# Batch 0's scaling on one engine, A^T in two steps, and one run of small tiles fewer, in a cross-attention and Gelu MLP kernel

## The chip, the cores and the metric

The kernel runs on one core of a Trainium2 chip. The metric is the time on the device in microseconds; the profile shows a single execution, and its times count from the start of that execution. The core's engines are named as in the profile: PE is TensorE (matrix products; PEld is its loading of weights), DVE is VectorE, ACT is ScalarE, POOL is GpSimd and SP is SyncE, which here only issues transfers.

## The reference

Two stages are computed. The first is cross-attention between x (8 batches, 8 heads, 512 rows of 64) and a state (32 rows of 64 for each head), in both directions. The second is an MLP with an exact Gelu on all rows of the result.

```python
scores = scale * np.matmul(x, state.transpose(0, 1, 3, 2))
a = softmax(scores)                       # written out: max, exp, sum, divide
xread = np.matmul(a, state)
scores2 = scale * np.matmul(state, x.transpose(0, 1, 3, 2))
a2 = softmax(scores2)
sread = np.matmul(a2, x)
attn = np.concatenate([xread, sread], axis=2)
# ... heads side by side: 4352 rows of 512
h = attn @ w_in                           # 512 x 2048
g = 0.5 * h * (1.0 + erf(h / sqrt(2)))
out = g @ w_out                           # 2048 x 512, float32
```

## The kernel before

xread is never formed. For each batch the kernel builds P, the product of the block-diagonal state (sbd) and w_in, and then takes `h = A @ P`, with A the scaled attention weights of all heads. P has 2 halves (t) by 2048 columns, built in chunks of 512 columns. The products of a chunk are small tiles: eight of 64x32, each with 512 columns. Everything else on TensorE uses the whole 128x128 array or has its own shapes.

The parts that matter here, cut; `...` marks cuts. The order of the calls is the order of the instructions on each engine.

```python
ps_f = ...tile_pool(name="ps_f", bufs=4, space=PSUM)     # tag "f": four PSUM banks in rotation
ps_o = ...tile_pool(name="ps_o", bufs=1, space=PSUM)     # tags o0 to o3: four banks, taken by turn

def otile(shape, name, at=None):
    if at is None:
        at = turn[0] % 4
        turn[0] += 1
    return ps_o.tile(shape, FP32, name=name, tag=f"o{at}")

def keep_warm(n):                       # products whose result nobody reads
    ps = otile([128, 512], "warm_ps")
    for _ in range(n):
        nc.tensor.matmul(ps[:, 0:128], lhsT=warm, rhs=warm, start=True, stop=True)

load_w_in(0, 256); load_w_in(256, 512)  # two transfers each, issued by GpSimd
load_w_out(0, 2); load_w_out(2, 4)
load_w_in(512, 1024)
load_st(1, 2)                           # state of batch 1

def norm0(t):                           # batch 0: A = e / sum, half t
    nc.vector.reciprocal(out=ics, in_=A.sums)
    eng = nc.gpsimd if t == 0 else nc.vector
    eng.tensor_tensor(out=..., in0=..., in1=ics..., op=ALU.mult)

def atr(b, ts=(0, 1)):                  # A^T through TensorE and PSUM
    ...
    for t in ts:
        ps = ps_f.tile([128, SJ, 128], BF16, name="aT_ps", tag="f")
        for j in range(SJ):
            nc.tensor.transpose(ps[:, j, :], A.a[:, 2 * j + t, :], ident)
        nc.vector.tensor_copy(out=A.AT[:, :, t, :], in_=ps)

def p_copy(b, f, ps):                   # a chunk of P: half 0 by ScalarE, half 1 by VectorE
    nc.scalar.copy(out=dst[:, 0, :], in_=ps[0])
    nc.vector.tensor_copy(out=dst[:, 1, :], in_=ps[1])

def pmat(b, f): ...                     # the products of one chunk, then p_copy
def burst(chunks): ...                  # the products of all chunks in one run, then the copies in order
def pmat00(h): ...                      # 256 columns of batch 0's chunk 0; both copies by ScalarE
def ones0(q): ...                       # VectorE copies for sread
def state_prep(b0, b1): ...             # transposes the states into sbd: TensorE, then VectorE
# M(m): two products A^T by P (line 481) and one Gelu by ScalarE
# mm2_m(0, m): four products g by w_out for batch 0 (line 534); U(u): four for later rows (line 507)

# the head
norm0(0); load_x(1); scores0(3); sums0(2); sums0(3); norm0(1)
load_rest()
keep_warm(2);  pmat00(0)
keep_warm(2);  pmat00(1)
nc.scalar.activation(out=gate, in_=gate, func=AF.Gelu)    # brings in the Gelu table early
keep_warm(10); atr(0, (0,))
keep_warm(3);  atr(0, (1,))
for q in range(4): ones0(q)
hps = [ps_f.tile(..., name="hp", tag="f") for m in range(4)]
for t in range(2):
    for m in range(4):
        nc.tensor.matmul(hps[m], lhsT=Ps[0][:, t, m*128:(m+1)*128], rhs=atts[0].AT[:, :, t, :], ...)
for m in range(4):
    nc.scalar.activation(out=gs[0][:, m, :], in_=hps[m], func=AF.Gelu)
turn[0] = 3
for m in range(3): mm2_m(0, m)
pmat(0, 1)
mm2_m(0, 3); M(4, 5); state_prep(1, 2); M(6)
...
pmat(0, 2) ... burst([(0, 3), (1, 0)]) ... burst([(1, 1), (1, 2)])
... burst([(1, 3), (2, 0), (2, 1)]) ... pmat(2, 2) ... pmat(2, 3)
```

After batch 2 the kernel goes through a steady loop, which the change leaves alone.

Of the kernel before, what the change touches and what calls it, by code (L numbers as in the profile page):

```python
# [10 lines left out]
BF16 = mybir.dt.bfloat16  # L11
# [6 lines left out]
def kernel(  # L18
# [8 lines left out]
    nc = tc.nc  # L27
# [8 lines left out]
    SJ = S // 128  # L36
# [11 lines left out]
    ps_f = ctx.enter_context(tc.tile_pool(name="ps_f", bufs=4, space=PSUM))  # L48
    ps_o = ctx.enter_context(tc.tile_pool(name="ps_o", bufs=1, space=PSUM))
# [3 lines left out]
    turn = [0]  # L53
# [6 lines that stand above are left out]
# [29 lines left out]
    for q in range(4):  # L89
        eng = nc.scalar if q == 2 else nc.sync  # L90
# [12 lines left out]
    def load_w_in(f0, f1):  # L103
        for t in range(2):
            nc.gpsimd.dma_start(  # L105
                out=w_in_bf[64 * t:64 * t + 64, :, f0:f1],
                in_=moe_w_in[256 * t:256 * t + 256, f0:f1].rearrange("(c d) f -> d c f", c=HC),
            )
# [3 lines left out]
    def load_w_out(m0, m1):  # L112
        nc.gpsimd.dma_start(out=w_out_bf[:, m0:m1, :], in_=w_out_r[:, m0:m1, :])
# [6 lines left out]
    def load_st(b0, b1):  # L120
        nc.gpsimd.dma_start(
            out=st_bf[:, b0:b1, :, :].rearrange("q b t d -> q (b t) d"),
            in_=st_rows[:, b0:b1, :, :].rearrange("q b t d -> q (b t) d"),
        )

    load_w_in(0, 256)
    load_w_in(256, 512)
    load_w_out(0, 2)
    load_w_out(2, 4)
    load_w_in(512, 1024)  # L130
    load_st(1, 2)


    def load_rest():
# [11 lines left out]
    def keep_warm(n):  # L146
# [5 lines that stand above are left out]
    def state_prep(b0, b1):  # L152
        n = b1 - b0
        ps = ps_f.tile([128, n, HC, NS], BF16, name="st_ps", tag="f")
        for b in range(b0, b1):
            nc.tensor.transpose(
                ps[:, b - b0, :, :].rearrange("p c n -> p (c n)"),
                st_bf[:, b, :, :].rearrange("q t d -> q (t d)"),
                ident,
            )  # L160
        for t in range(2):
            nc.vector.tensor_copy(
                out=sbd[64 * t:64 * t + 64, b0:b1, :, 32 * t:32 * t + 32].rearrange(
                    "d b c n -> d (b c) n"
                ),
                in_=ps[64 * t:64 * t + 64, :, :, :].rearrange("d b c n -> d (b c) n"),
            )
# [76 lines left out]
    def ones0(q):  # L244
        nc.vector.tensor_copy(
            out=atts[0].xo[:, :, q % 2 * 2:q % 2 * 2 + 2, 2 + q // 2 * 64:66 + q // 2 * 64],
            in_=x0b[:, q, :, :, :],
        )
# [58 lines left out]
    def norm0(t):  # L307
        A = atts[0]
        ics = att.tile([128, SJ, HC], FP32, name="ics", tag="ics")
        nc.vector.reciprocal(out=ics, in_=A.sums)  # L310
        eng = nc.gpsimd if t == 0 else nc.vector
        eng.tensor_tensor(
            out=A.a.rearrange("p (j t) (c n) -> p j t c n", t=2, n=NS)[:, :, t, :, :],
            in0=A.e.rearrange("p (j t) (c n) -> p j t c n", t=2, n=NS)[:, :, t, :, :],
            in1=ics[:, :, :].to_broadcast((128, SJ, HC, NS)),
            op=ALU.mult,
        )
# [39 lines left out]
    def atr(b, ts=(0, 1)):  # L357
        A = atts[b]
        if 0 in ts:
            A.AT = att.tile([128, SJ, 2, 128], BF16, name="AT", tag="AT")  # L360
        for t in ts:
            ps = ps_f.tile([128, SJ, 128], BF16, name="aT_ps", tag="f")
            for j in range(SJ):
                nc.tensor.transpose(ps[:, j, :], A.a[:, 2 * j + t, :], ident)
            nc.vector.tensor_copy(out=A.AT[:, :, t, :], in_=ps)

    def atr_dma(b):
        A = atts[b]
# [6 lines left out]
    def sread(b):  # L375
        A = atts[b]
        A.sr = ftile([128, 2, 65], "sr")
        for t in range(2):
            for j in range(SJ):
                for c in range(HC):  # L380
                    nc.tensor.matmul(  # L381
                        A.sr[32 * c:32 * c + 32, t, :],
                        lhsT=A.e[:, 2 * j + t, 32 * c:32 * c + 32],
                        rhs=A.xo[:, j, c, 1 + 65 * t:66 + 65 * t],
                        start=(j == 0),
                        stop=(j == SJ - 1),
                    )

    def sread_out(b):
        A = atts[b]  # L390
        A.srm = att.tile([128, 2, D], BF16, name="srm", tag="srm")
        flat = A.sr.rearrange("q t d -> q (t d)")
        inv = att.tile([128, 2], FP32, name="inv", tag="inv")
        nc.vector.reciprocal(out=inv, in_=flat[:, 0:130:129])
        nc.vector.tensor_tensor(
            out=A.srm,
            in0=flat[:, 1:129].rearrange("q (t d) -> q t d", t=2),
            in1=inv[:, :].to_broadcast((128, 2, D)),
            op=ALU.mult,
        )  # L400
# [11 lines left out]
    def p_mm(b, f, tiles):  # L412
        if b not in Ps:
            Ps[b] = att.tile([128, 2, d_ff], BF16, name="P", tag="P")
        ps = [tiles([128, 512], "p_ps") for t in range(2)]
        for c in range(HC):
            for t in range(2):
                nc.tensor.matmul(  # L418
                    ps[t][32 * c:32 * c + 32, :],
                    lhsT=sbd[64 * t:64 * t + 64, b, c, 32 * t:32 * t + 32],  # L420
                    rhs=w_in_bf[64 * t:64 * t + 64, c, f * 512:(f + 1) * 512],
                    start=True,
                    stop=True,
                )
        return ps

    def p_copy(b, f, ps):
        dst = Ps[b][:, :, f * 512:(f + 1) * 512]
        nc.scalar.copy(out=dst[:, 0, :], in_=ps[0])  # L429
        nc.vector.tensor_copy(out=dst[:, 1, :], in_=ps[1])  # L430

    def pmat(b, f):
        p_copy(b, f, p_mm(b, f, ftile))
# [4 lines left out]
    def burst(chunks, b_read=None):  # L438
        done = []
        first = len(chunks) < 4 and b_read is not None  # L440
        if first:
            sread(b_read)
        for i, (b, f) in enumerate(chunks):
            done.append((b, f, p_mm(b, f, ftile if i < 2 else otile)))
        for x in done[:2]:
            p_copy(*x)
        if b_read is not None and not first:
            sread(b_read)
        for x in done[2:3]:
            p_copy(*x)  # L450
        if b_read is not None:
            sread_out(b_read)
        for x in done[3:]:
            p_copy(*x)
# [75 lines left out]
    def mm2_m(b, m):  # L530
        for j in range(SJ):
            if m == 0:
                ops[b, j] = otile([128, d_model], "op")
            nc.tensor.matmul(  # L534
                ops[b, j],
                lhsT=gs[b][:, m, j * 128:(j + 1) * 128],
                rhs=w_out_bf[:, m, :],
                start=(m == 0),
                stop=(m == MC - 1),
            )  # L540
# [268 lines left out]
    def M(*ms):  # L809
        for m in ms:  # L810
            mm1(m // MC, m % MC)

    def U(*us):
        for u in us:
            mm2(u // 16, u % 16 // 4, u % 4)
# [28 lines left out]
    load_rest()  # L844
    keep_warm(2)
    pmat00(0)
    keep_warm(2)
    pmat00(1)
    nc.scalar.activation(out=gate, in_=gate, func=AF.Gelu)
    keep_warm(10)  # L850
    atr(0, (0,))
    keep_warm(3)
    atr(0, (1,))
    for q in range(4):
        ones0(q)

    gs[0] = gpool.tile([128, MC, S], BF16, name="g", tag="g")
    hps = [ps_f.tile([128, S], FP32, name="hp", tag="f") for m in range(4)]  # L860
    for t in range(2):
        for m in range(4):
            nc.tensor.matmul(  # L863
                hps[m],
                lhsT=Ps[0][:, t, m * 128:(m + 1) * 128],
                rhs=atts[0].AT[:, :, t, :],
                start=(t == 0),
                stop=(t == 1),
            )
    for m in range(4):  # L870
        nc.scalar.activation(out=gs[0][:, m, :], in_=hps[m], func=AF.Gelu)
    turn[0] = 3
    for m in range(3):
        mm2_m(0, m)
    pmat(0, 1)
    mm2_m(0, 3)
    M(4, 5)
    state_prep(1, 2)
    M(6)
    begin(1)  # L880
    xtr(1, (0, 1))
# [18 lines left out]
    M(10, 11)  # L900
    mm2_m(0, 8)
    mm2_m(0, 9)
    burst([(0, 3), (1, 0)])
    mm2_m(0, 10)
    atr(1)
    M(12, 13)
# [5 lines left out]
    xtr_dma(2)  # L912
    rearr_ones(2)
    U(12)
    burst([(1, 1), (1, 2)])
    U(13)
    state_prep(2, B)
    M(16, 17)
    U(14)
    M(18, 19)  # L920
    U(15)
    burst([(1, 3), (2, 0), (2, 1)])
    U(16)


# [2 lines left out]
    nc.gpsimd.tensor_copy(out=hold, in_=gs[1][:, 4, 0:1])  # L928
    load_x(4)
    w_sums(0)  # L930
    pmat(2, 2)
    begin(3)
    rearr(3)
    xtr_dma(3)
# [97 lines left out]
    b = B - 1  # L1032
# [40 lines left out]
```

The softmax here doesn't subtract the row's maximum and nothing guards it: scores larger than these inputs give would overflow.

## Time and profile before

| | |
|---|---|
| time, median of 3 runs | 206.2 us (206.19 to 206.49) |
| profiled execution | 205.62 us, span 203.8 us |
| busy: PE, DVE, ACT, POOL | 97%, 66%, 65%, 32% of the span |
| granted TensorE clock | 1.00 |
| scaling of batch 0, half 0 (POOL) | 9.08 us, 1.09 long |
| scaling of batch 0, half 1 (DVE) | 9.44 us, 1.28 long |
| the eight hp products of batch 0's first chunk | from 11.39 us |
| first Gelu | 12.66 us |

The profile lists, for each engine, what it did and when, and what ended the idle time ahead of an instruction. The chain of work that ended last is followed back from the end: at each step to whatever released it. Where that chain is on one engine without a gap, only less work on this engine, or an earlier start, makes the kernel shorter. The ends of matrix products are modelled, so the distance between the starts of groups says more than the length of one product.

### The profile page before, as it was taken

How to read it: one execution, taken by the hardware profiler on the slowest of the kernel's cores; microseconds unless marked ns; L12 is line 12 of the kernel's file. 1: busy time of each engine (PE TensorE's matmuls, PEld its weight loads, DVE VectorE, ACT ScalarE, POOL GpSimd, SP SyncE). 2: the span in 40 equal slices, each digit the busy share in tenths (PEclk: the TensorE clock that was granted, in tenths of full speed). 3: DMA queues.
4: the chain of work that ended last, by engine and by line, in shares of the span. 5: the costliest groups of instructions: out<-in, count | busy, mean ns of one | idle time of the engine just before them, and what ended most of it. 6: DMA issues, size and time to landing. Idle time of an engine off the chain costs nothing.

```text
span 203.8 us, 4714 instructions
## 1 busy us (share of the span) xinstructions
PE 197.9 (97%) x1972; PEld 131.2 (64%) x1979; DVE 134.0 (66%) x219; ACT 133.3 (65%) x240; POOL 65.9 (32%) x73
## 2 busy tenths in 40 slices
PE   8799999999999999999999999999999999999994
PEld 7445444444444577766776687567775887778893
DVE  2944675776758649876797767765778543165883
ACT  3774875589894879566967596678857376744120
POOL 8984610755060315360527502420220011200000
PEclk9999999999999999999999999999999999999999
DMA  6999999789575908782783306340109001030125
GB/s 195 192 176 202 206 199 193 127 236 124 127 96 155 204 11 106 156 180 29 89 170 142 69 0 140 124 102 3 53 37 172 3 0 51 3 154 0 55 100 159
DMA packets 40325, 23.14 MB, mean 114 GB/s; under 512 B 21872, under 2 KB 38384, under 8 KB 40304
## 3 DMA queue, kind: packets, MB, share of 16 engines
q1 hardware_dynamic: 25616, 14.36, 29.2%
q0 software_dynamic: 14000, 8.10, 29.1%
q10 hardware_dynamic: 688, 0.39, 0.6%
q8 instruction: 15, 0.25, 0.5%
q14 instruction: 6, 0.05, 0.1%
HBM read 17.30 MB, written 8.91 MB: 129 GB/s over the span
## 4 chain that ended last, share of the span: by engine, by line
PE 93%; DMA 2%; POOL 2%; issue 0%; DVE 0%; POOLq 0%
PE xp L589 35%; PE hp L481 27%; PE op L507 8%; PE op L534 5%; PE p_ps L418 5%; PE hps L521 3%; PE rp L765 3%; DMA w_in_bf<-in_moe_w_in_dram 2%; PE xp L695 2%; PE pt L327 2%; PE sr L381 1%; POOL w_in_bf L105 1%; PE hp L863 1%; POOL sbd L95 1%; PE xT_ps L267 1%
## 5 line engine op out<-in xcount | busy, mean ns | idle before, releaser
L488 ACT ACTIVATE g<-hp 128x512 bf16<-128x512 f32 x124 | 67.0, 602 | 27.4 <-PE hp L481 21.9
L481 PE MATMUL hp<-AT,P 128*128 128x512 bf16 x248 | 63.6, 379 | 0.1
L589 PEld LDWEIGHTS <-gsum 128*128 128x128 bf16 x448 | 43.4, 98 | 11.1 <-issue 1.9
L583 DVE TENSOR_TENSOR gsum<-g 128x2048 bf16<-128x2048 bf16 x30 | 38.6, 1307 | 0.1
L481 PEld LDWEIGHTS <-P 128*128 128x128 bf16 x248 | 22.8, 98 | 20.8 <-issue 2.5
L589 PE MATMUL xp<-ws,gsum 128*128 128x256 bf16 x256 | 30.6, 273 | 0.0
L430 DVE CAST P<-p_ps 128x512 bf16<-128x512 f32 x31 | 20.1, 686 | 10.6 <-PE p_ps L418 10.5
L589 PE MATMUL xp<-ws,g 128*128 128x256 bf16 x192 | 22.9, 273 | 0.0
L589 PE MATMUL xp<-w_out_bf,gsum 128*128 128x256 bf16 x192 | 22.8, 273 | 0.0
L429 ACT CAST P<-p_ps 128x512 bf16<-128x512 f32 x31 | 16.9, 597 | 7.4 <-PE p_ps L418 7.2
L589 PEld LDWEIGHTS <-g 128*128 128x128 bf16 x192 | 18.8, 98 | 4.3
L638 POOL TENSOR_TENSOR u<-s,oh 128x512 f32<-128x512 f32 x5 | 6.6, 1311 | 41.0 <-ACT oh L635 41.0
L507 PE MATMUL op<-w_out_bf,g 128*128 128x512 bf16 x76 | 19.0, 379 | 0.1
L231 POOL COPY xo<-xb 128x1024 bf16<-128x1024 bf16 x12 | 14.5, 1240 | 12.6 <-PE sr L381 12.6
L221 POOL COPY x<-xb 128x1024 bf16<-128x1024 bf16 x12 | 12.3, 1056 | 8.5 <-DMA xb<-in_x_dram 8.5
L608 POOL TENSOR_TENSOR v<-q,oh 128x512 f32<-128x512 f32 x5 | 7.1, 1428 | 20.8 <-ACT oh L640 20.8
L507 PEld LDWEIGHTS <-g 128*128 128x128 bf16 x80 | 7.6, 98 | 9.6 <-issue 0.8
L347 DVE TENSOR_REDUCE cs<-e 128x16 f32<-128x512 bf16 x14 | 9.5, 678 | 3.4 <-ACT e L334 3.4
L534 PE MATMUL op<-w_out_bf,g 128*128 128x512 bf16 x45 | 11.4, 380 | 0.2
L632 DVE TENSOR_TENSOR s<-xp,s 128x512 f32<-128x512 f32 x5 | 3.5, 692 | 11.3 <-PE xp L589 11.3
L350 DVE TENSOR_TENSOR a<-e,ics 128x512 bf16<-128x512 bf16 x14 | 10.3, 738 | 0.5
L418 PE MATMUL p_ps<-w_in_bf,sbd 64*32 64x512 bf16 x248 | 10.4, 382 | 0.1
(111 smaller groups left out, 220.3 us busy)
## 6 DMA issues: line engine op xcount, KB each, us to landing
xb<-in_x_dram POOLq DMA_DIRECT2D x7, 512.0 KB, 7.4
out_dram<-oh SPq DMA_DIRECT2D x13, 256.0 KB, 2.4
out_dram<-osb SPq DMA_DIRECT2D x10, 256.0 KB, 3.4
out_dram<-oh SPq DMA_DIRECT2D x5, 512.0 KB, 2.8
w_out_bf<-in_moe_w_out_dram POOLq DMA_DIRECT2D x8, 256.0 KB, 9.7
w_in_bf<-in_moe_w_in_dram POOLq DMA_DIRECT2D x6, 256.0 KB, 10.1
x0f<-in_x_dram SPq DMA_DIRECT2D x3, 256.0 KB, 3.8
w_in_bf<-in_moe_w_in_dram POOLq DMA_DIRECT2D x4, 128.0 KB, 4.1
```

What stands on the lines that cost most here:

```text
L221: nc.gpsimd.tensor_copy(out=A.x4[:, :, :, 64 * t:64 * t + 64].rearrange("p j c d -> p c j d"), in_=src[:, t],)
L231: eng.tensor_copy(out=A.xo[:, :, :, 2 + 64 * t:66 + 64 * t].rearrange("p j c d -> p c j d"), in_=src[:, t],)
L350: nc.vector.tensor_tensor(out=A.a[:, :, hs].rearrange("p g (c n) -> p g c n", n=NS), in0=e4, in1=ics[:, :, :].to_broadcast((128, G, 2, NS) ...
L418: nc.tensor.matmul(ps[t][32 * c:32 * c + 32, :], lhsT=sbd[64 * t:64 * t + 64, b, c, 32 * t:32 * t + 32], rhs=w_in_bf[64 * t:64 * t + 64, c ...
L429: nc.scalar.copy(out=dst[:, 0, :], in_=ps[0])
L430: nc.vector.tensor_copy(out=dst[:, 1, :], in_=ps[1])
L481: nc.tensor.matmul(hp, lhsT=Ps[b][:, t, m * 128:(m + 1) * 128], rhs=atts[b].AT[:, :, t, :], start=(t == 0), stop=(t == 1),)
L488: nc.scalar.activation(out=gs[b][:, m, :], in_=hp, func=AF.Gelu)
L507: nc.tensor.matmul(ps, lhsT=gs[b][:, m, j * 128:(j + 1) * 128], rhs=w_out_bf[:, m, :], start=(m == 0), stop=(m == MC - 1),)
L534: nc.tensor.matmul(ops[b, j], lhsT=gs[b][:, m, j * 128:(j + 1) * 128], rhs=w_out_bf[:, m, :], start=(m == 0), stop=(m == MC - 1),)
L583: nc.vector.tensor_tensor(out=t, in0=g_q(b, h0, k0), in1=g_q(b, h1, k1), op=op)
L589: nc.tensor.matmul(ps[:, j - js[0], :], lhsT=lhs[:, m, 128 * j:128 * j + 128], rhs=rhs[:, m, :], start=(first and j == js[0] and m == 0), ...
```

## The change

The multiplication for half 0 of batch 0's scaling moves from GpSimd to VectorE, so both halves are done there, one behind the other. The first half of A^T is transposed ahead of pmat00(1), into a bank of ps_o, and copied by ScalarE. The four products of half 0 come before the second half's transposes, which then stand between the two halves of products. The warming products are divided anew. Batch 1's state is loaded and prepared earlier, so that batch 1's first P chunk can be built in the same run of small tiles as batch 0's second; the later chunks move up by one place each, and the run for (2,2) alone falls away. The number of chunks, products and copies of P stays the same.

```diff
     load_w_in(256, 512)
+    load_st(1, 2)
     load_w_out(0, 2)
     load_w_out(2, 4)
     load_w_in(512, 1024)
-    load_st(1, 2)
@@ norm0
-        eng = nc.gpsimd if t == 0 else nc.vector
-        eng.tensor_tensor(
+        nc.vector.tensor_tensor(
@@ atr
-            ps = ps_f.tile([128, SJ, 128], BF16, name="aT_ps", tag="f")
+            if b == 0:
+                ps = ps_o.tile([128, SJ, 128], BF16, name="aT_ps", tag=f"o{turn[0] % 4}")
+                turn[0] += 1
+            else:
+                ps = ps_f.tile([128, SJ, 128], BF16, name="aT_ps", tag="f")
             ...
-            nc.vector.tensor_copy(out=A.AT[:, :, t, :], in_=ps)
+            copy = nc.scalar.copy if b == 0 and t == 0 else nc.vector.tensor_copy
+            copy(out=A.AT[:, :, t, :], in_=ps)
@@ the head
     pmat00(0)
-    keep_warm(2)
+    keep_warm(5)
+    atr(0, (0,))
+    keep_warm(4)
     pmat00(1)
     nc.scalar.activation(out=gate, in_=gate, func=AF.Gelu)
-    keep_warm(10)
-    atr(0, (0,))
     keep_warm(3)
-    atr(0, (1,))
-    for q in range(4):
-        ones0(q)
     ...
     for t in range(2):
+        if t == 1:
+            keep_warm(6)
+            atr(0, (1,))
+            keep_warm(4)
+            for q in range(4):
+                ones0(q)
         for m in range(4):
             nc.tensor.matmul(hps[m], ...)
@@ batch 0 and 1
-    for m in range(3):
-        mm2_m(0, m)
-    pmat(0, 1)
+    mm2_m(0, 0)
+    state_prep(1, 2)
+    mm2_m(0, 1)
+    mm2_m(0, 2)
+    burst([(1, 0), (0, 1)])
     mm2_m(0, 3)
     M(4, 5)
-    state_prep(1, 2)
     M(6)
     ...
-    burst([(0, 3), (1, 0)])
+    burst([(0, 3), (1, 1)])
     ...
-    burst([(1, 1), (1, 2)])
+    burst([(1, 2), (1, 3)])
     ...
-    burst([(1, 3), (2, 0), (2, 1)])
+    burst([(2, 0), (2, 1), (2, 2)])
     ...
-    pmat(2, 2)
```

## The prediction

> **What bounds the kernel now.** I read the page's busy times first, then the chain of work that ended last in order of time, and then the timeline of the first microseconds engine by engine. The page says that TensorE is nearly all there is:
>
> ```profile
> PE 197.9 (97%) x1972; PEld 131.2 (64%) x1979; DVE 134.0 (66%) x219; ACT 133.3 (65%) x240; POOL 65.9 (32%) x73
> ```
>
> The chain (start, length, engine, tile) says where it is not:
>
> ```profile
> 5.05 4.59 DMA w_in_bf<-in_moe_w_in_dram
> 9.68 0.30 PE p_ps L463 x7
> 9.98 0.66 PE warm_ps L149 x10
> 10.65 0.24 PE aT_ps L364 x4
> 10.91 0.44 DVE AT L365
> 11.39 1.89 PE hp L863 x8
> 13.32 0.39 PE op L534
> ...
> 16.08 0.34 PE p_ps L418 x8
> 16.42 0.97 PE op L534 x4
> 17.39 0.86 PE hp L481 x4
> ...
> 29.22 0.61 PE p_ps L418 x16
> 29.83 0.97 PE op L534 x4
> ```
>
> Two things are to be seen. From 11.39 us on the chain stays on TensorE almost without a break: four 128x512 products take 0.86 us, 0.215 us each, group after group. So a later engine or transfer gains nothing there unless it held TensorE, and whatever shifts that start shifts the end by as much. And a run of small tiles (p_ps) has a fixed price: alone, 0.34 us, and the four op products behind it take 0.97 instead of 0.86, so 0.45 us in all; two chunks in one run cost 0.61 + 0.11 = 0.72 us. The second chunk of a run thus costs 0.27 us, and a lone one 0.45.
>
> Ahead of 11.39 the timelines of VectorE, GpSimd and ScalarE matter (start, length, engine, line; the 50.10 line is a later scaling of the same size with no GpSimd work beside it):
>
> ```profile
> 9.08 1.09 POOL L312 TENSOR_TENSOR a<-e,ics 128x512 bf16<-128x512 bf16 x1
> ```
> ```profile
> 9.44 1.28 DVE L312 TENSOR_TENSOR a<-e,ics 128x512 bf16<-128x512 bf16 x1
> 10.91 0.82 DVE L365 COPY AT<-aT_ps 128x512 bf16<-128x512 bf16 x2 [0.18 <-PE aT_ps L364]
> ...
> 50.10 0.69 DVE L350 TENSOR_TENSOR a<-e,ics 128x512 bf16<-128x512 bf16 x1
> ```
> ```profile
> 8.65 0.65 ACT L471 CAST P<-p_ps 128x256 bf16<-128x256 f32 x2
> 10.04 0.65 ACT L471 CAST P<-p_ps 128x256 bf16<-128x256 f32 x2 [0.74 <-PE p_ps L463]
> 10.71 1.28 ACT L849 ACT_TABLE_LOAD   x1
> ...
> 12.66 1.58 ACT L871 ACTIVATE g<-hp 128x512 bf16<-128x512 f32 x3 [0.46 <-PE hp L863]
> ```
>
> The first half of the scaled A is ready at 9.08 + 1.09 = 10.17, the second at 9.44 + 1.28 = 10.72. The eight hp products go in the order t=0 (four), t=1 (four), so the fifth, which completes the first hp, starts at 11.39 + 0.86 = 12.25, and the first Gelu follows 0.41 us later, at 12.66. ScalarE had been free for 0.46 us then.
>
> **What the Trainium skill says.** "SBUF — State Buffer", section "Who interferes with whom": a VectorE instruction with two SBUF inputs contends with a GpSimd one that reads SBUF. The trace agrees: 1.28 us beside GpSimd's 1.09, against 0.69 alone. "TensorEngine Tiling (Array Packing)", section "Key Properties": changing the tiling mode drains TensorE. The 0.34 + 0.11 us of a lone run, against 0.27 for a second chunk in a run, fit that. "ScalarE activation tables: per-element evaluation and per-set limits": functions in different sets are one table load of 1283 ns apart; here it is 1.28, and it sits behind the P copies on ScalarE's queue, so a copy put ahead of it moves it.
>
> **Part 1, the scaling.** The GpSimd multiplication goes away. VectorE has the first reciprocal done at 8.26 + 0.25 = 8.51 (the timeline of before), so its first multiplication runs from 8.55 to 9.24 at 0.69 us: the first half of A is ready 0.93 us earlier. The price is on the second half: two reductions (0.69 together before), a reciprocal (0.25) and the second multiplication (0.69), with some 0.05 between, end near 10.9 us instead of 10.72.
>
> **Part 2, A^T and its products in two steps.** I follow the new order of TensorE, with a transposition of four tiles from start to the copy's start at 0.45 us (10.48 to 10.91 before), and 0.056 us for a warming product (ten in 0.56).
> - First transposes at 9.24 + 0.08 = 9.32. ScalarE copies them from 9.77; a copy of 128x512 bf16 from PSUM took it 0.59 us early in the run, so it ends at 10.36.
> - pmat00(1) starts at about 9.85 (its weights came at 9.68 before), but its two copies stand behind the A^T copy on ScalarE: 10.36 to 11.0 instead of 10.04 to 10.69. The table load and the gate follow, so Gelu could start at 11.0 + 1.28 + 0.21 = 12.5; that is still ahead of 12.66.
> - The three warming products ahead of the first hp products use the PSUM bank of the first transposes (the fourth turn after it), and so wait for the same ScalarE copy: 10.42 to 10.59. The four t=0 products run from 10.59 to 11.45, against 11.39 to 12.25 before: 0.8 us ahead.
> - Then six warming products, 0.34 us, to 11.79. The second half of A has been ready since 10.9, so these are on the path. Second transposes 11.79; VectorE's copy from 12.23 to 12.64; the first t=1 product at 12.70.
>
> Before, that product started at 12.25. So the head loses 0.45 us: the 0.86 us of products that were moved ahead are paid for by a transposition, a copy and six warming products that now stand between the halves and were beside other work before. From 12.70 the rest follows as before: first Gelu 13.1, mm2 some 0.66 later.
>
> **Part 3, the P chunks.** Seven runs carried eleven chunks (1, 1, 2, 2, 3, 1, 1); now six do (2, 1, 2, 2, 3, 1). One lone run at 0.45 becomes a second chunk at 0.27: -0.2 us. Batch 0's own chunk is now the second of its run, so its copies come behind those of (1,0). In the run at 29.22 the second VectorE copy ended 1.77 us after the run's start, and TensorE has 0.72 + 0.86 us of work until then; M(4)'s t=0 product covers the rest but some 0.05 us: +0.05.
>
> **Part 4, the loads.** The small state load goes ahead of w_out, and GpSimd issues x[1] about 0.9 us earlier. DMA engines are 90% busy there, so an earlier issue lands little earlier. The w_in half for chunk (0,1) comes last: the GpSimd issue that waited for it went on at 16.24, hard on the use at 16.08. It may land 0.2 us later now, and is used 0.27 + 0.45 later. I count nothing.
>
> **Sum.** +0.45 + 0.05 - 0.2 = +0.3 us: 206.5.
>
> **Rivals.**
> - *The head gains.* If VectorE's second multiplication were really late, the six warming products would cost nothing; and without them and with no wait on ScalarE the second transposes could start at 11.0 and the t=1 products at 11.95, 0.3 us ahead of before, limited by ScalarE's 12.5 to a gain of about 0.15. With the run saved: 205.85. For it speaks that 0.8 us of products do move ahead; against it that the order on TensorE is fixed and the warming products stand in it.
> - *The head stays as it was*, because the A^T copy or the semaphores are faster than I take them, and only the run is saved: 206.0.
> - *The head is worse*: the table load behind a later P copy, VectorE's scaling slowed by GpSimd's descriptor work (1.28 instead of 0.69 twice): second half of A at 12.0, t=1 products at 13.0, 206.8.
> - *The w_in half lands late*, and the two-chunk run waits for it: up to 0.3 us on top.
>
> **Range and chances.** My sum gives 206.5; the first two rivals are likelier together than the last two, and I take 0.1 off: 206.4. The range 205.8 to 206.9 runs from the first rival to the third. The largest effect is a quarter of one per cent, so within 2% has 0.98, and 0.01 stands on each side.
>
> **What would show it.** In the profile after: no GpSimd multiplication; two VectorE multiplications of 0.69 us, the first from about 8.55; the first t=0 product near 10.6, and the second group of hp products near 12.7 (this decides part 2; at 12.25 or less I am wrong); first Gelu at 13.1; the run of sixteen small tiles near 16.5 with 0.72 us in place of 0.45; one lone run fewer near 43.5; every later group moved by the same amount, +0.3 at 60 us. I would be wrong in kind if TensorE had a wait after 13 us that is not there now, above all for w_in at 16 to 17 us.

## The result, and the profile after

The changed kernel took 206.77 us (median of 4 runs, 206.47 to 207.2) against 206.24 us: a ratio of 1.0025, interval 1.0001 to 1.0049. A second series of 22 runs gave 206.58 us and 1.0020 (1.0005 to 1.0034). So it is slower by about 0.2%, or 0.4 us. Single executions of the kernel before spread over 3 us, from 205.3 to 208.3, and those of the changed one from 206.0 to 207.3, so a pair of profiles has to be taken apart before it says anything.

The busy times in the page after:

```profile
PE 198.9 (97%) x1979; PEld 132.1 (65%) x1986; DVE 133.7 (65%) x219; ACT 133.8 (65%) x241; POOL 63.9 (31%) x72
```

The chain of work that ended last, after, in order of time (pieces of 0.05 us and less left out):

```profile
9.59 0.41 PE aT_ps L367 x4
10.03 0.59 ACT AT L369
10.66 0.33 PE warm_ps L149 x3
10.99 0.86 PE hp L867 x4
11.85 0.34 PE warm_ps L149 x6
12.19 0.24 PE aT_ps L367 x4
12.45 0.43 DVE AT L369
12.92 1.04 PE hp L867 x4
13.99 0.39 PE op L538
...
16.81 0.56 PE p_ps L422 x16
17.36 0.97 PE op L538 x4
18.34 1.50 PE hp L485 x6
19.85 1.01 PE xT_ps L267 x32
...
51.89 3.12 DMA AT<-a
55.06 1.04 PE hp L485 x4
```

The head is laid out as predicted, step by step: transposes, ScalarE's copy, three warming products behind it, four products, six warming products, transposes, VectorE's copy. The second group starts at 12.92. The scaling is as predicted too (VectorE's timeline, after):

```profile
8.56 0.25 DVE L310 RECIPROCAL ics<-cs 128x16 f32<-128x16 f32 x1
8.84 0.69 DVE L311 TENSOR_TENSOR a<-e,ics 128x512 bf16<-128x512 bf16 x1
...
10.51 0.69 DVE L311 TENSOR_TENSOR a<-e,ics 128x512 bf16<-128x512 bf16 x1
```

The spans of the two profiles differ by 0.9 us (204.7 and 203.8). Fixed points on TensorE say where: 0.30 us are there at the first reciprocal (8.56 against 8.26), ahead of every edited instruction; 0.37 us come between it and the fifth hp product (4.36 against 3.99 us); from the first mm2 product to batch 1's transposes it is +0.35 (17.83 against 17.48), of which 0.27 is the chunk that moved ahead; from there to the end of the hp group behind batch 2's A^T it is -0.17 (24.28 against 24.45). The rest of the span is the same, 148.6 us in both. So behind the head the changed kernel is 0.18 us longer, where the prediction had it 0.15 shorter.

Two waits are new. One is at M(4), whose products come right behind the four op products that follow the two-chunk run. From the start of these op products to the first hp product it takes 1.04 us, and 0.88 before:

```profile
17.30 1.04 PE L538 MATMUL op<-w_out_bf,g 128*128 128x512 bf16 x4
18.34 1.50 PE L485 MATMUL hp<-AT,P 128*128 128x512 bf16 x6
```

before:

```profile
16.35 1.04 PE L534 MATMUL op<-w_out_bf,g 128*128 128x512 bf16 x4
17.23 1.03 PE L481 MATMUL hp<-AT,P 128*128 128x512 bf16 x4
```

PEld, TensorE's loading of weights, shows why: the weights of the first product wait for ScalarE's copy of P, the second of its run. Those of the second wait for VectorE's, but that costs little: 0.25 us between the two products in place of 0.215. Together the wait is 0.2 us.

```profile
18.34 0.10 PEld L485 LDWEIGHTS <-P 128*128 128x128 bf16 x1 [0.50 <-ACT P L433]
18.59 0.55 PEld L485 LDWEIGHTS <-P 128*128 128x128 bf16 x4 [0.16 <-DVE P L434]
```

The other is the AT line at 51.89 in the chain: TensorE waits about 0.2 us for the transposing transfer of batch 2's A.

### The profile page after: what moved, and what is told of

It reads as the page before. It is cut to its first block, busy times and chain, and to the rows that moved or that the text cites. A ratio compares the mean times of both kernels' runs of the same rounds, so it can differ in the third digit from the quotient of the medians.

```text
span 204.7 us, 4727 instructions
## 1 busy us (share of the span) xinstructions
PE 198.9 (97%) x1979; PEld 132.1 (65%) x1986; DVE 133.7 (65%) x219; ACT 133.8 (65%) x241; POOL 63.9 (31%) x72
## 4 chain that ended last, share of the span: by engine, by line
PE 90%; ACT 4%; DVE 2%; DMA 2%; issue 1%
PE xp L593 34%; PE hp L485 25%; PE op L511 6%; PE op L538 5%; PE p_ps L422 4%; PE hps L525 3%; PE rp L769 3%; PE warm_ps L149 2%; PE xp L699 2%; ACT g L492 2%; DMA AT<-a 2%; PE pt L326 1%; PE sr L385 1%; PE hp L867 1%; ACT L492 1%; ACT L333 1%
```

## The experiments

Theory A was mine: TensorE bounds everything from the head on, the reordered head costs 0.45 us and the saved run gives 0.2 back. B: the order of the loads makes the loss. C: the saved run is given back at batch 2's A^T. D: the arrival of w_in bounds the stretch from 16 to 31 us, whatever the head does. Ratios are against the kernel before on the same chip, with their 95% interval. They are not the quotients of the two medians, and at this size the two can disagree: the chunks alone give 1.0003 and 1.0017, the kernel without warming products 0.9991 and 1.0014. Differences between versions of 0.1% are not settled by either.

**The kernel before again.** No edit.

> The kernel before, unchanged, for its spread: in the profiled execution of the changed kernel everything was already 0.30 us late at 8.3 us, ahead of the first changed instruction on TensorE. If that lateness is chance from one execution to the next, this profile may have its first reciprocal (line 310) anywhere from 8.26 to 8.6 us. If the earlier state load causes it, this one stays at 8.26. Time 206.2 to 206.3 in either case.

206.17 us, 1.0004 (0.9987 to 1.0022). The late start came back in the unchanged kernel: its first reciprocal was at 8.71 us, so the 0.30 us of the first pair is no work of the change. On TensorE's timeline, the kernel before in its first profile:

```profile
4.74 0.39 PE L253 MATMUL xT_ps<-ident,x0b 128*128 128x128 bf16 x4
```

and in this one:

```profile
4.92 0.63 PE L253 MATMUL xT_ps<-ident,x0b 128*128 128x128 bf16 x4
...
15.95 0.81 PE L418 MATMUL p_ps<-w_in_bf,sbd 64*32 64x512 bf16 x8
```

The four transposes of the start took 0.63 us for 0.39. And in spite of the late reciprocal the first hp product came at 11.33 us, no later than the 11.39 of the first profile: the old head is not tied to the scaling. The second line is a lone run of small tiles; here TensorE waited 0.4 us in it for w_in. In the first profile nothing was missing:

```profile
16.01 0.41 PE L418 MATMUL p_ps<-w_in_bf,sbd 64*32 64x512 bf16 x8
```

**The chunks alone.**

```diff
 (before) load_st(1, 2) ahead of w_out; the runs of small tiles and state_prep as in the change; old head
```

> The kernel before with the run of small tiles saved and the state load moved ahead, but with the old head. Theory A (the reordered head costs the time, the saved run gains 0.2 us): 206.0, TensorE 0.2 us ahead from 45 us on. Rival B (the earlier state load delays the start and x[1]): 206.5 to 206.7, first reciprocal near 8.56 and a wait for x[1] near 19 us. Rival C (the saved run is given back where batch 2's transposed A arrives, near 55 us): 206.2, with a TensorE wait for that transfer of about 0.2 us.

206.52 us against 206.16, 1.0003 (0.9985 to 1.0021): no gain, and a loss not excluded. The late reciprocal that B expected isn't there (8.28 us); C's wait is. On VectorE's timeline near 48 us, and TensorE's at 54:

```profile
48.34 1.08 DVE L350 TENSOR_TENSOR a<-e,ics 128x512 bf16<-128x512 bf16 x1
```
```profile
54.34 1.04 PE L481 MATMUL hp<-AT,P 128*128 128x512 bf16 x4 [0.20 <-DMA AT<-a]
```

With the lone run gone, batch 2's scores come 0.4 us earlier against GpSimd's copies of x[3], and the scaling falls beside them: 1.08 us in place of 0.69. This is the contention of two engines for SBUF that the prediction met in the head, moved to another place. From batch 1's transposes to the group behind A^T it took 24.29 us against 24.45: of the 0.45 us that the lone run had cost there, 0.29 were lost again, and the chunk had been paid for ahead.

**The head alone.**

```diff
 (changed) loads, runs of small tiles and state_prep as before
```

> The changed kernel's head (both scalings on VectorE, A^T in two steps) with the old loads and chunks. Theory A: 206.65, the first product of the second half at 12.7 us against 12.25 before, and later groups late by the same 0.4 us. Rival B: 206.2, as the loads are the old ones.

206.27 us, 0.9997 (0.9976 to 1.0018). The second group starts at 13.11 us, 4.37 us behind its reciprocal as in the changed kernel, and yet no loss is measured, though up to 0.4 us lies within the interval. In this profile no run of small tiles waits for w_in. Of the two profiles of the kernel before, one has no such wait either, and the other 0.4 us near 16 us and more behind it.

**No warming products around the first half's products.**

```diff
-    keep_warm(3)
@@
-            keep_warm(6)
```

> The changed kernel without the three and the six warming products around the first half's products. Theory A: the second transposes start 0.5 us earlier (at 11.5 against 12.0 in the profile after), Gelu at 12.85, and the time falls by 0.4 to 0.5 us, to 206.3. Rival D (x[1] lands near 19.4 us whatever TensorE does): TensorE reaches its transposes at 19.1, waits there, and the time stays within 0.1 us of 206.77.

206.45 us, 0.9991 (0.9971 to 1.0010). The second group starts at 12.53, 3.87 us behind the reciprocal in place of 4.36: the 0.5 us are there. The median stands above that of the kernel before and the ratio below 1, so the time is not settled. Behind the head, the profile shows 0.1 us of wait in the run at 16.3 us, 0.2 in the one at 24.6 and 0.5 at A^T.

**The changed kernel again.** No edit.

> The changed kernel, unchanged, with more executions, because single executions of either kernel spread over 2 us. If the loss of 0.25% from four executions is the kernel's own, this gives 1.002 to 1.003 again. If the loss in the head is made up where TensorE waits for w_in anyway (16 to 31 us), it gives 1.000 to 1.001.

The second series above: 1.0020 (1.0005 to 1.0034). The loss is the kernel's own. (The spread of 2 us that the expectation gives to both kernels holds for the kernel before alone.)

**Eighteen more warming products.**

```diff
-            keep_warm(6)
+            keep_warm(24)
```

> The changed kernel with 24 warming products in place of 6 ahead of the second transposes: 18 more at 0.056 us, 1.0 us more on TensorE in the head. If TensorE bounds the whole of the run from the head on (theory A), the time rises by 1.0 us over the changed kernel, to 207.4 to 207.8. If the arrival of w_in, w_out and x[1] bounds the stretch from 16 to 31 us (rival D), part is absorbed there: a rise of 0.3 to 0.7 us.

207.46 us, 1.0060 (1.0041 to 1.0079): 0.88 us above the changed kernel of the same series (206.58), of 1.0 us added. So with the change the head is on the path, and lateness beyond its own isn't absorbed. Chain of this kernel:

```profile
11.86 1.34 PE warm_ps L149 x24
13.20 0.24 PE aT_ps L367 x4
```

**GpSimd's copies of x[3] later.**

```diff
-    rearr_ones(3)
@@ batch 2, first step
         nc.gpsimd.tensor_copy(out=hold, in_=gs[b][:, 0, 0:1])
+        if b == 2:
+            rearr_ones(3)
```

> The changed kernel with GpSimd's copies of x[3] into xo moved behind batch 2's first Gelu, so that no GpSimd read lies beside VectorE's scaling of batch 2 near 49 us. In the changed kernel that multiplication took 1.06 us in place of 0.69, and TensorE waited 0.2 us for the transposed A at 55 us. If the contention is the cause (theory C): 0.69 us again, the transfer is issued some 0.35 us earlier, the wait at 55 us is gone, and the time falls by 0.2 us. If another thing holds the transfer (the transposing transfer of x[3] ahead of it in the queue): the multiplication is shorter and the wait stays.

206.58 us, 1.0022 (1.0005 to 1.0038): no gain. The scaling is back at 0.69 us, but the wait grew to 0.3 us. SyncE's queue:

```profile
48.02 4.21 SPq L274 DMA_TRANSPOSE xT<-x  x1
52.41 1.23 SPq L374 DMA_TRANSPOSE AT<-a  x1
```

The transfer of x[3] stands ahead of A's, and A's is issued only when it is through.

**Both, without warming products.** The edits of the two runs together.

> The changed kernel without the three and six warming products and with those GpSimd copies moved. Theory A and C together: 0.5 us less in the head and 0.2 to 0.5 us less at 55 us, 205.9 to 206.1, faster than the kernel before. If w_in's arrival bounds the middle: 206.2 to 206.3.

206.29 us, 0.9994 (0.9967 to 1.0021): no difference from the kernel before is shown. In its profile, a long execution of 207.58 us, the transfer of x[3] held the queue for 5.28 us and TensorE waited 1.4 us for A^T.

**A's transfer first.**

```diff
-    xtr_dma(3)
@@
     atr_dma(2)
+    xtr_dma(3)
     (and GpSimd's copies of x[3] later)
```

> The changed kernel with GpSimd's copies of x[3] moved as in the run before and the transposing transfer of x[3] put behind that of batch 2's A in SyncE's queue. In the profiles so far this queue held A back when x[3] took over 3.9 us (4.2 and 5.3 us: waits of 0.3 and 1.4 us on TensorE). Theory C, both causes gone: A's transfer is issued near 51.6 us, no wait at 55 us, 0.2 to 0.4 us less than the changed kernel's 206.58: 206.2 to 206.4. Rival: x[3] now comes late for its scores near 58 us, and the wait moves there: no gain.

206.56 us, 1.0025 (1.0001 to 1.0048). The wait is gone from the profile; the time isn't measurably better. So C names a real wait of 0.2 us, and it isn't what makes the loss.

**Everything mended, new head.** No warming products, A's transfer first, and:

```diff
     mm2_m(0, 3)
+    sread(0)
+    sread_out(0)
     M(4, 5)
```

> The changed kernel without its nine warming products, with A's transfer freed, and with batch 0's sread products put ahead of M(4), where TensorE now waits 0.21 us for the P copies of the two-chunk run. Sum of the parts: 206.58 - 0.5 - 0.3 - 0.2 = 205.6. If TensorE then waits for w_in in the runs of small tiles (rival D): 205.9 to 206.2, with those runs longer than 0.56 us for sixteen tiles.

206.6 us, 1.0021 (1.0002 to 1.0040), where the parts summed to 205.6 and D had 206.2 at most. TensorE's timeline has the answer:

```profile
12.14 1.02 PE L865 MATMUL hp<-AT,P 128*128 128x512 bf16 x4 [0.29 <-DVE AT L369]
...
15.96 0.60 PE L422 MATMUL p_ps<-w_in_bf,sbd 64*32 64x512 bf16 x9
17.00 0.41 PE L422 MATMUL p_ps<-w_in_bf,sbd 64*32 64x512 bf16 x7 [0.44 <-DMA w_in_bf<-in_moe_w_in_dram]
...
26.11 0.41 PE L422 MATMUL p_ps<-w_in_bf,sbd 64*32 64x512 bf16 x7 [0.66 <-DMA w_in_bf<-in_moe_w_in_dram]
```

The head is 0.8 us earlier than in the profile after (its reciprocal too came early, at 8.27), and TensorE stands in the middle of the run and waits for w_in, twice. That is theory D, for a head this early; for the late head of the changed kernel the added warming products speak against it. This execution was a long one, 207.48 us, so the waits of a usual one may be smaller.

**Everything mended, old head.** The chunks alone, with A's transfer first and sread ahead of M(4).

> The kernel before's head with the saved run, A's transfer freed and the sread products ahead of M(4). Theory: the saved run's 0.23 us is now kept, 205.9 against 206.15 for the kernel before. Rival D (w_in's arrival bounds 16 to 31 us): within 0.1 us of the kernel before.

206.47 us against 205.87, 1.0017 (0.9997 to 1.0036). The gain that the theory expected isn't there, and D's 0.1 us is exceeded. In its profile the run at 15.90 us ends at 17.85, 1.95 us for 0.62.

**The order of the loads alone.**

```diff
+    load_st(1, 2)
     load_w_out(0, 2)
     load_w_out(2, 4)
     load_w_in(512, 1024)
-    load_st(1, 2)
```

> The kernel before with nothing changed but the order of the loads: batch 1's state ahead of w_out. GpSimd's wait for the second half of w_in 512 to 1024 ended at 16.2 to 16.7 us in the three profiles with the old order and at 16.6 to 17.7 us in ten with the new. Theory D (the new order delays w_in by 0.6 us): the lone run of small tiles near 16 us takes 0.3 to 0.9 us longer than 0.41, and the time rises by 0.2 to 0.5 us over the kernel before. Rival: the later w_in comes from the other edits; the wait ends by 16.6 again, and the time is that of the kernel before.

206.6 us, 1.0025 (1.0006 to 1.0044). This one line moved is measured at what the whole change costs. So the time speaks for B, but it isn't shown: three other kernels with the same line moved measured no loss (the chunks alone 1.0003, the two without warming products 0.9991 and 0.9994), though their intervals don't exclude one.

As to the way, the profile bears out only part of the expectation. The lone run took 0.2 us longer, where 0.3 to 0.9 was expected:

```profile
16.23 0.60 PE L418 MATMUL p_ps<-w_in_bf,sbd 64*32 64x512 bf16 x8
```

A two-chunk run at 29.5 us took 0.15 longer, the first hp product came at 11.61 (11.16 to 11.39 in the other old heads), and TensorE waited 0.6 us for A^T, with the lone run still in its place; the transposing transfer of x[3] had held SyncE's queue for 4.97 us there. The kernel before, with the old order, waited more for w_in than this one in its second profile: 0.4, 0.2 and 0.6 us in three runs.

Why w_in is late with the new order is to be seen where GpSimd issues it. In the kernel before, w_in's two transfers are issued in front of the state's:

```profile
7.13 1.26 POOL L105 DMA_DIRECT2D w_in_bf<-in_moe_w_in_dram  x2
8.36 0.74 POOL L121 DMA_DIRECT2D st_bf<-in_state_dram  x1
```

With the loads alone the state's is issued at 5.60 us, ahead of w_out's two, and w_in's two follow at:

```profile
7.71 1.31 POOL L105 DMA_DIRECT2D w_in_bf<-in_moe_w_in_dram  x2
```

To issue the state's 32 KB takes GpSimd 0.74 us, about as much as 256 KB of w_out or w_in take it (0.61 to 0.74), and the issue of w_in starts 0.6 us later: at 7.13 to 7.18 us in the three profiles with the old order, at 7.70 to 7.87 in the eleven with the new one. GpSimd's timeline shows when it could go on behind w_in's second half; here:

```profile
16.67 0.63 POOL L105 DMA_DIRECT2D w_in_bf<-in_moe_w_in_dram  x1 [0.80 <-DMA w_in_bf<-in_moe_w_in_dram]
```

in the kernel before:

```profile
16.24 0.71 POOL L113 DMA_DIRECT2D w_out_bf<-in_moe_w_out_dram  x1 [1.52 <-DMA w_in_bf<-in_moe_w_in_dram]
```

and after the change:

```profile
17.15 0.63 POOL L105 DMA_DIRECT2D w_in_bf<-in_moe_w_in_dram  x1 [0.29 <-DMA w_in_bf<-in_moe_w_in_dram]
```

Over all profiles the end of this wait is 16.24, 16.60 and 16.65 us with the old order, and 16.63 to 17.69 us, 17.1 on average, in the eleven with the new one, so 0.6 us later on average, like the issue; the ranges touch, and the kernel with the loads alone lies where they do. What it does to TensorE depends on when it comes there:

| kernel | loads | fifth hp product | run of small tiles starts | tiles | GpSimd behind w_in | run longer by |
|---|---|---|---|---|---|---|
| before | old | 12.25 | 16.01 | 8 | 16.24 | 0 |
| before again | old | 12.19 | 15.95 | 8 | 16.60 | 0.40 |
| head alone | old | 13.11 | 16.87 | 8 | 16.65 | 0 |
| loads alone | new | 12.47 | 16.23 | 8 | 16.67 | 0.19 |
| chunks alone | new | 12.02 | 15.84 | 16 | 16.63 | 0.33 |
| after | new | 12.92 | 16.74 | 16 | 17.15 | 0 |
| after again | new | 13.07 | 16.88 | 16 | 17.35 | 0.01 |
| 18 more warming products | new | 13.94 | 17.75 | 16 | 16.97 | 0.01 |
| copies of x[3] later | new | 13.05 | 16.87 | 16 | 17.48 | 0.15 |
| A's transfer first | new | 13.05 | 16.86 | 16 | 17.24 | 0.01 |
| no warming products | new | 12.53 | 16.34 | 16 | 16.90 | 0.10 |
| both, no warming products | new | 12.47 | 16.28 | 16 | 16.66 | 0.01 |
| all mended, new head | new | 12.14 | 15.96 | 16 | 17.25 | 0.83 |
| all mended, old head | new | 12.08 | 15.90 | 16 | 17.69 | 1.33 |

(Fifth product of the old head: its first plus 0.86. Longer than 0.41 us for eight tiles and 0.62 for sixteen, with the idle time within.) One rule of this table fits every row within 0.02 us: the run is longer by what w_in's landing lies behind the run's start, less 0.25 us for eight tiles or 0.46 for sixteen, and by nothing where that is negative. So a late head mostly meets no wait, and an early one waits. No version is shown to be faster than the kernel before.

## Why the prediction was right, and where not

The total was right: 206.4 with a range of 205.8 to 206.9, against 206.77 and 206.58. Several of its terms were not, and that they summed to nearly the measured loss is partly luck: in the pair of profiles the saved run's gain was missing, and the loads, which alone measured as much as the whole, had no term.

- **The scaling.** Right: 0.69 us twice, no multiplication on GpSimd.
- **The head, +0.45 us.** The new chain was right: reciprocal to second group takes 4.36 to 4.37 us in all five profiles with it, and 12.70 against 8.51 in the prediction is 4.19 behind the reciprocal's end, or 4.44 behind its start. It is on the path there, as the added warming products show. The old head was taken wrongly. I took it as bound by the scaled A, as in the one profile that I had. In five profiles its fifth product lies 3.41 to 3.99 us behind the reciprocal, at 12.0 to 12.5 us whether the reciprocal is at 8.26 or 8.71. It starts behind w_in and ten warming products, as the chain that I had shown says; the change ties it to the scaling. In profiles with a late reciprocal the new head is therefore 0.45 to 0.97 us behind the old one.
- **The head's effect on the end.** Here the step "from 12.70 the rest follows as before" failed. The head alone is 0.9997 (0.9976 to 1.0018). The second profiles of the two kernels show how a late head can cost nothing: the first mm2 product starts at 13.26 us before and 14.13 after, and yet the spans are 204.9 and 204.8, since the kernel before then takes 18.43 us to batch 1's transposes, with waits for w_in in three runs of small tiles, and the changed one 17.66 with none. What the prediction read as TensorE's chain "almost without a break" was, in these profiles, a tie between TensorE and the loads.
- **The saved run, -0.2 us.** Right for TensorE by itself. Of it, the wait at M(4), put at 0.05 us, took 0.2. The prediction reckoned with VectorE's copy of P, which the second product waits for, and that part came true (0.04 us); it passed over ScalarE's, which holds the first product by 0.16. And the wait at A^T, 0.2 us, wasn't seen at all; it is the kind of wait behind 13 us that the prediction said would show it wrong.
- **The loads, "I count nothing".** By the run of the loads alone, the wrong term. I put w_in 0.2 us later, and took it that an earlier or later issue moves the landing little. Both issue and landing came 0.6 us later on average over the kernels with the new order, and the loads alone cost 0.25% (0.06 to 0.44%), 0.1 to 0.9 us where the sum had nothing. In the changed kernel's profile the cover holds, because its head is late; that also fits that mending the head showed no gain over the kernel before. The rival "the w_in half lands late" was the right one to keep, with too small a size.

The parts don't add: loads alone 0.25%, head alone 0, the whole 0.2%. Two limits that end close to each other, TensorE and the loads, would do that: the later one counts and not the sum. This is argued from the table and from the added warming products; the intervals alone, each 0.3 to 0.4% wide, would let the parts add as well. What stays open is whether the loads cost as much in the changed kernel as alone, and how the 0.25% arise there: one profile of that kernel shows several small delays and no large one. In the changed kernel GpSimd also issued the transfers behind x[1] up to 1.2 us earlier, and x[1] itself, issued at 8.93 us in place of 10.08, was waited for until 19.63 in place of 18.94. Why it came later wasn't tried alone.

## What to carry to other kernels

A chain that stays on one engine in one profile doesn't show that this engine bounds the stretch: look at how hard on their use the loads land, and take a second profile of the same kernel, before gains are added up. A small load can push back large ones behind it by more than its bytes suggest, since its issue takes GpSimd as long as theirs (0.74 us for 32 KB here); put it behind the last of those that the next step waits for. And an operation that comes earlier can fall beside one that it didn't meet before, or behind a transfer in a queue: ask what each earlier start collides with.

## What the runs showed that I had not expected

The start itself varies by up to 0.45 us between executions of the same kernel: the first reciprocal of the kernel before at 8.26 or 8.71 us. The first four transposes at 4.7 to 5.0 us take 0.39 us in five profiles, 0.51 in one and 0.63 in eight. The Trainium skill, "TensorE: Matmul & The Clock Gate", section "What's actually happening", says that the clock is released by a window that runs freely and doesn't start with the kernel; durations that differ like this would fit that, but no run here moved the window. It isn't the whole of it either: in two profiles the transposes took 0.39 us and the reciprocal was late all the same (8.67 and 8.69 us), where TensorE had waited 0.92 us in all for the casts of x[0], against 0.49 in the first profile. And the transposing transfer of x[3], the same size each time, held SyncE's queue for 3.2 to 5.3 us when issued at 46 to 49 us, and for 1.9 us when issued at 53 to 54 us, behind A's. A wait behind such a transfer has no fixed size.
